# Top-k attention and capped experts on one core: mask products ahead of the second score products, and the signed-score product moved from GpSimd to VectorE

## The chip, the cores and the metric

One core of one Trainium2 chip runs the whole program. TensorE (PE) multiplies matrices, VectorE (DVE) searches and compares, ScalarE (ACT) evaluates exponentials and signs and copies out of PSUM, GpSimd (POOL) does elementwise work on SBUF, SyncE (SP) issues the DMAs. The metric is the device time of one execution in microseconds. The median of the runs is compared; the profile is of one execution.

## The reference

Attention over 8 batches, 8 heads, 576 positions and head size 64, in which each row keeps only its 32 largest scores, followed by a layer of 8 experts that each take at most 80 tokens.

```python
scores = scale * np.matmul(q, k.transpose(0, 1, 3, 2))            # 8 x 8 x 576 x 576
kth = np.partition(scores, -top_k, axis=-1)[..., -top_k:-top_k + 1]   # top_k = 32
scores = np.where(scores >= kth, scores, -1e9)
attn = np.exp(scores - scores.max(-1)); attn /= attn.sum(-1) + 1e-09
x = matmul(attn, v)                                               # -> (4608, 512)
logits = x @ w_gate; expert_idx = argmax(logits); gate_w = softmax(logits)[expert_idx]
for e in range(8):                                                # at most 80 tokens each, by gate_w
    out[tok_idx] = gate_w[tok_idx] * (np.maximum(x[tok_idx] @ w1[e], 0) @ w2[e])
```

## The kernel before

The attention works through 32 head pairs (two heads of one batch, side by side in the 128 partitions as 64 + 64). The 576 query rows of a pair are four blocks of 128 rows and a tail of 64. A unit is one head's block of 128 rows; the tail rows of both heads share one unit. So a pair has nine units, and the attention has 288. `run` issues one step for each unit in a fixed order (`manual_schedule`: each engine executes its instructions in the order written). Within a step the work of several units is staggered:

- `front` (lines 180 to 195): PE computes the score products of a block of both heads (line 190), ACT copies them out of PSUM as `s` (line 195). It is issued two steps ahead of its use.
- `parts` (line 202): six MAX8 over sixths of a row give 48 candidates.
- `search`: three rounds of MAX8 (line 213) and two of MATCH_REPLACE (line 222) on the candidates give the 24th largest, `w9[:, 7]`. ACT then computes the sign of (that value minus s), with its sum over the row in `cnt` (line 218). GpSimd multiplies s by that sign (line 219), which makes the scores above the 24th negative. A MAX8 of the product (line 224) gives the eight next ones, and `pick` (line 227) takes the 32nd by the count.
- `drop` (line 249): VectorE writes `mask`, 1 where s is below the threshold, plus a constant of the row, in bf16.
- `turn_w` (lines 252 to 273): PE computes the scores a second time, transposed (keys by queries, line 269, f32, one head in partitions 0 to 63 and the other in 64 to 127), on top of a product of the mask with a scaled negative identity (line 265, bf16, all 128 partitions), which adds a very large negative number where the key is dropped. The sums lie in PSUM tiles `ab` (four chunks of 128 keys for each head) and `cc` (the last 64 keys of both heads). ACT then takes the exponential of it (lines 272 and 273) as `wT`. In the order before, each chunk of 128 keys has its two mask products and then its two score products, and then the next chunk follows.
- `back` (line 287): PE multiplies `wT` with the values; ACT copies the result out (line 289).
- `norm` (lines 293 to 331) divides, stores, transposes and multiplies with the gate's weights, once in a head pair. GpSimd does the division's products (line 304).

Within a step the order of VectorE's instructions is written as a string, `"GbGcGdGehGmGga"`. G is one of the six `parts` MAX8 of the step's own unit; every other letter is the next piece of `search` of a unit that the table `back` places 0 to 3 steps behind: b to e the rounds (1 step behind), g the MAX8 of the product (2 behind), h and m `pick` and the mask (3 behind). After VectorE's string the step issues `turn_w` of the block whose mask has just been written, then `front` (or the transposes of the next pair's q and k), then `back` of an earlier block. These three share PE in that order, and `front`'s PSUM tile `sp` and `turn_w`'s `ab` have one buffer each. After the attention `judge` tests a bound and `finish` routes the tokens and runs the experts; the change does not touch them.

Of the kernel before, what the change touches and what calls it, by code (L numbers as in the profile page):

```python
# [14 lines left out]
Alu = mybir.AluOpType  # L15
# [9 lines left out]
def kernel(  # L25
# [11 lines left out]
    nc = tc.nc  # L37
    B, H, S, D = q.shape
# [8 lines left out]
    P = 128  # L47
    HP = H // 2
    NP = B * HP
    NF = S // P  # L50
    TL = S - NF * P
    NK = NF + 1
# [60 lines left out]
    class Attention:  # L113
# [92 lines left out]
        def search(self, i):  # L206

            s, cand = self.s[i], self.top[i]
            top = self.top[i] = self.small.tile([P, G0 // 8 - 1, 8], F32, name="top", tag="top")
            w9 = self.small.tile([P, 16], F32, name="w9", tag="w9")  # L210
            for r in range(G0 // 8):
                dst = top[:, r, :] if r < G0 // 8 - 1 else w9[:, :8]
                nc.vector.max(out=dst, in_=cand)  # L213
                if r == G0 // 8 - 1:

                    y = self.rows.tile([P, S], F32, name="y", tag="y", bufs=3)
                    cnt = self.small.tile([P, 1], F32, name="cnt", tag="cnt")
                    nc.scalar.activation(y, s, Act.Sign, bias=w9[:, 7:8], scale=-1.0, accum_out=cnt)  # L218
                    nc.gpsimd.tensor_tensor(out=y, in0=s, in1=y, op=Alu.mult)  # L219
                yield  # L220
                if r < G0 // 8 - 1:
                    nc.vector.match_replace(out=cand, in_to_replace=dst, in_values=cand, imm_value=LOW)  # L222
                    yield
            nc.vector.max(out=w9[:, 8:], in_=y)  # L224
            yield
            pick = self.small.tile([P, TOP_K - G0 + 1], F32, name="pick", tag="pick")
            nc.vector.scalar_tensor_tensor(out=pick, in0=past, scalar=cnt, in1=w9[:, 7:], accum_out=self.thr[:, i : i + 1],  # L227
                                           op0=Alu.is_equal, op1=Alu.mult)
            yield
            self.drop(i)  # L230
            yield
# [19 lines left out]
        def turn_w(self, n, t):  # L251

            qT, kT = self.turned[n]
            i = n * UPP + 2 * t
            m = P if t < NF else TL
            masks = [self.mask.pop(i), self.mask.pop(i + 1)] if t < NF else [self.mask.pop(i)] * 2
            eye = [minus, minus] if t < NF else [minus[:, :TL], minus[:, TL:]]
            ab = self.ps_w.tile([P, 2, NF, P], F32, name="ab", tag="ab")
            cc = self.ps_c.tile([P, 512], F32, name="cc", tag="cc")
            rows = slice(t * P, t * P + m)  # L260
            for c in range(NK):
                ks = slice(c * P, min(c * P + P, S))
                for h in range(2):
                    d = slice(D * h, D * h + D)
                    nc.tensor.matmul(ab[:, h, c, :m] if c < NF else cc[d, :m], lhsT=masks[h][:, ks], rhs=eye[h],  # L265
                                     start=True, stop=False)
                for h in range(2):
                    d = slice(D * h, D * h + D)
                    nc.tensor.matmul(ab[:, h, c, :m] if c < NF else cc[d, :m], lhsT=kT[d, ks], rhs=qT[d, rows],  # L269
                                     start=False, stop=True)  # L270
            wT = self.rows.tile([P, 2 * NF + 1, P], F32, name="wT", tag="wT")
            nc.scalar.activation(wT[:, : 2 * NF, :m], ab.rearrange("p h c r -> p (h c) r")[:, :, :m], Act.Exp, scale=scale)  # L272
            nc.scalar.activation(wT[:, 2 * NF, :m], cc[:, :m], Act.Exp, scale=scale)
            self.w[n, t] = wT, cc
# [93 lines left out]
        def run(self, slow):  # L368

            units = []  # L370
            for n in range(NP):
                for t in range(NF):
                    units += [(n, t, 0), (n, t, 1)]
                units.append((n, NF, 2))
            first, second = {}, {}
            later = []
            due = []

            def step(i):
                if i < NU:  # L380
                    n, t, h = units[i]
                    if t == 0 and h == 1 and 0 < n and n + 1 < NP:
                        self.load(n + 1, *divmod(n + 1, HP))
                    if t in (1, 3) and h == 0 and slow and n:
                        slow.pop(0)()
                    if t == 1 and h == 0 and n + 1 < NP:
                        due.append(n + 1)
                    first[i] = self.parts(i)

                back = dict(a=0, b=1, c=1, d=1, e=1, g=2, h=3, m=3)  # L390
                for c in "GbGcGdGehGmGga":
                    if c == "G":
                        if i < NU:
                            next(first[i])
                    elif c == "a":
                        if i < NU:
                            next(first[i], None)
                            second[i] = self.search(i)
                            next(second[i])
                    elif i - back[c] in second:  # L400
                        next(second[i - back[c]])
                j = i - 3
                if 0 <= j < NU and units[j][2]:
                    self.turn_w(*units[j][:2])
                self.fronts = i + 2 < NU and units[i + 2][2] != 1
                if self.fronts:
                    self.front(*units[i + 2][:2])
                elif due:
                    self.turn(due.pop())
                j = i - 4  # L410
                if 0 <= j < NU and units[j][2]:
                    self.back(*units[j][:2])
                for g in list(later):
                    if next(g, 0) == 0:
                        later.remove(g)
                if 0 <= j < NU and units[j][2] == 2:
                    n = units[j][0]
                    b, hp = divmod(n, HP)
                    later.append(self.norm(n, b, hp, b % 2, 2))

            with tc.manual_schedule():
                self.load(0, 0, 0)
                self.load(1, *divmod(1, HP))
                nc.sync.dma_start(wg, moe_w_gate.rearrange("(c p) e -> p c e", p=P))
                self.turn(0)
                self.front(0, 0)
                i = 0
                while i < NU + 4 or later:
                    step(i)
                    i += 1  # L430
            assert not slow and not due
# [273 lines left out]
```

## Time and profile before

| | before |
|---|---|
| median of 3 runs | 1617.32 us (1616.72 to 1620.83) |
| profiled execution | 1612.21 us, span 1610.5 us |
| PE busy | 1311.5 us, 81% of the span |
| VectorE busy | 1124.7 us, 70% |
| ScalarE busy | 682.4 us, 42% |
| GpSimd busy | 513.0 us, 32% |
| mean granted TensorE clock | 0.826 |

Busy time is the time in which an engine has an instruction under way; waiting is not counted. The granted clock is given as a share of full speed: 1.0 is 2.4 GHz, 0.5 is 1.2 GHz. A timeline row has the start in us from the span's start, the duration in us, the engine, the line of the kernel, the operation, the tiles written and read with their shapes, the number of merged instructions, and in brackets the idle time before it with what ended it. A row of waits has the waiting engine and line, what it waited for, the total in us, the number of waits and the longest. A row of a window has the stretch, its length, the busy time of PE, PE's weight loads, DVE, ACT and POOL with the numbers of instructions, the granted clock, the share of the DMA engines and GB/s.

### The profile page before, as it was taken

The page shows a single profiled execution, that of the slowest core. Times are in us where ns is not written, and L with a number is a line of the kernel's source. Part 1 is how long each engine was busy: PE and PEld are TensorE (multiplying, and loading weights), DVE is VectorE, ACT ScalarE, POOL GpSimd, SP SyncE. Part 2 cuts the span into 40 slices and gives each one's busy share as a digit, 9 for nine tenths or more (in the row PEclk, how much of TensorE's full clock was granted, in tenths as well). Part 3 has the DMA queues.
Part 4 walks back from the last instruction along what each step waited for, and adds up shares of the span by engine and source line. Part 5 has one row for each costly group of instructions (what it writes and reads, how often), then busy time and mean ns, then how long its engine had stood idle before and what let it go on. Part 6 is the DMA issues. An engine that isn't in the chain of part 4 may idle for free.

```text
span 1610.5 us, 38356 instructions
## 1 busy us (share of the span) xinstructions
PE 1311.5 (81%) x14862; PEld 936.5 (58%) x14862; DVE 1124.7 (70%) x5095; ACT 682.4 (42%) x1374; POOL 513.0 (32%) x501
## 2 busy tenths in 40 slices
PE   6889888888888888888888888888888888861787
PEld 4556555555555665555555556655555556550687
DVE  5777777777777777786777777777877777838211
ACT  3454444444444544444444445444444444420010
POOL 2333333333333333333333332333333333320111
PEclk9888788887888887888878888878888788775699
DMA  4022222222111122222221111111111110021270
GB/s 119 9 76 83 83 69 57 57 57 57 38 43 42 49 57 56 57 57 57 57 57 32 46 29 26 31 31 31 31 31 31 31 31 9 9 73 39 74 289 25
DMA packets 154591, 85.94 MB, mean 53 GB/s; under 512 B 118304, under 2 KB 136736, under 8 KB 154400
## 3 DMA queue, kind: packets, MB, share of 16 engines
q1 hardware_dynamic: 153376, 80.78, 17.6%
q0 software_dynamic: 1024, 2.62, 0.5%
q8 instruction: 118, 1.93, 0.5%
q14 instruction: 73, 0.60, 0.1%
HBM read 63.19 MB, written 20.19 MB: 52 GB/s over the span
## 4 chain that ended last, share of the span: by engine, by line
PE 70%; DVE 17%; ACT 11%; issue 2%; POOL 0%; DMA 0%; POOLq 0%; DVEq 0%; ACTq 0%
PE ab L269 19%; PE sp L190 15%; PE ab L265 9%; PE cc L287 9%; ACT s L195 5%; DVE mask L249 4%; DVE cand L202 4%; PE cc L269 4%; DVE pick L227 3%; PE sp L165 3%; PE lp L322 2%; PE yp L613 2%; ACT wT L272 2%; DVE cand L222 2%; PE cc L265 2%
## 5 line engine op out<-in xcount | busy, mean ns | idle before, releaser
L219 POOL TENSOR_TENSOR y<-s,y 128x576 f32<-128x576 f32 x288 | 416.7, 1447 | 891.9 <-ACT y L218 888.1
L202 DVE MAX8 cand<-s 128x8 f32<-128x96 f32 x1728 | 428.7, 248 | 253.2 <-ACT s L195 253.1
L269 PE MATMUL ab<-qT,kT 64*128 64x128 f32 (+1 forms) x2560 | 359.2, 363 | 0.0
L272 ACT ACTIVATE wT<-ab 128x1024 f32<-128x1024 f32 (+1 forms) x160 | 150.2, 939 | 415.8 <-PE ab L269 413.7
L265 PE MATMUL ab<-minus,mask 128*128 128x128 bf16 (+1 forms) x1280 | 197.8, 233 | 150.7 <-DVE mask L249 132.2
L190 PE MATMUL sp<-kT,qT 64*128 64x288 f32 (+1 forms) x1280 | 275.3, 565 | 48.3 <-ACT s L195 25.7
L224 DVE MAX8 w<-y 128x8 f32<-128x576 f32 x288 | 214.6, 745 | 92.9 <-POOL y L219 92.9
L269 PEld LDWEIGHTS ab<-qT,kT 64*128 64x128 f32 x2560 | 228.1, 218 | 68.5 <-issue 18.5
L249 DVE TENSOR_SCALAR mask<-s,thr,top 128x576 bf16<-128x576 f32 x288 | 264.9, 920 | 0.3
L265 PEld LDWEIGHTS <-mask 128*128 128x128 bf16 (+1 forms) x1600 | 103.8, 104 | 255.7 <-DVE mask L249 145.7
L287 PEld LDWEIGHTS cc<-vb,wT 128*64 128x64 f32 x4608 | 210.5, 163 | 67.2 <-issue 52.7
L195 ACT ACTIVATE s<-sp 128x1152 f32<-128x1152 f32 (+1 forms) x160 | 165.7, 1035 | 181.0 <-PE sp L190 180.8
L287 PE MATMUL cc<-vb,wT 128*64 128x65 f32 x4608 | 241.6, 251 | 0.0
L218 ACT ACTIVATE y<-s,w 128x576 f32<-128x576 f32 x288 | 222.8, 774 | 18.7 <-DVE w L213 18.6
L190 PEld LDWEIGHTS sp<-kT,qT 64*128 64x128 f32 (+1 forms) x1280 | 140.6, 233 | 128.9 <-ACT s L195 55.8
L227 DVE SCALAR_TENSOR_TENSOR pick<-past,cnt,w 128x9 f32<-128x9 f32 x288 | 140.4, 487 | 0.2
L222 DVE MATCH_REPLACE8 cand<-top,cand 128x48 f32<-128x48 f32 x576 | 110.2, 191 | 0.0
L213 DVE MAX8 top<-cand 128x8 f32<-128x48 f32 x576 | 110.0, 191 | 0.1
L287 PE MATMUL cc<-vr,wT 128*64 128x65 f32 x1152 | 101.8, 245 | 0.0
L269 PE MATMUL cc<-qT,kT 64*64 64x128 f32 (+1 forms) x640 | 79.7, 335 | 0.0
L289 ACT COPY xu<-cc 128x130 f32<-128x130 f32 (+1 forms) x160 | 42.3, 265 | 80.2 <-PE cc L287 80.1
L287 PEld LDWEIGHTS cc<-vr,wT 128*64 128x64 f32 x1152 | 74.8, 161 | 0.0
(165 smaller groups left out, 991.3 us busy)
## 6 DMA issues: line engine op xcount, KB each, us to landing
w<-in_moe_w_dram SPq DMA_DIRECT2D x32, 512.0 KB, 4.5
w<-in_moe_w_dram SPq DMA_DIRECT2D x8, 2048.0 KB, 11.9
out_dram<-zero SPq DMA_DIRECT2D x9, 1024.0 KB, 8.3
qn<-in_q_dram SPq DMA_DIRECT2D x64, 128.0 KB, 2.7
kn<-in_k_dram SPq DMA_DIRECT2D x64, 128.0 KB, 2.7
vb<-in_v_dram SPq DMA_DIRECT2D x64, 128.0 KB, 2.4
xd<-xn SPq DMA_DIRECT2D x32, 256.0 KB, 2.4
qn<-in_q_dram SPq DMA_DIRECT2D x32, 32.0 KB, 2.5
```

The lines of the kernel that those rows point to most:

```text
L190: nc.tensor.matmul(o, lhsT=qT[d, t * P : t * P + m], rhs=kT[d, j * HS : (j + 1) * HS], start=True, stop=True)
L195: nc.scalar.activation(s[:, : g * S].rearrange("p (j c) -> p j c", c=HS), ps[:, : 2 * g, :HS], Act.Copy, scale=TINY)
L202: nc.vector.max(out=cand[:, j, :], in_=s[:, j * S // NG : (j + 1) * S // NG])
L218: nc.scalar.activation(y, s, Act.Sign, bias=w9[:, 7:8], scale=-1.0, accum_out=cnt)
L219: nc.gpsimd.tensor_tensor(out=y, in0=s, in1=y, op=Alu.mult)
L224: nc.vector.max(out=w9[:, 8:], in_=y)
L227: nc.vector.scalar_tensor_tensor(out=pick, in0=past, scalar=cnt, in1=w9[:, 7:], accum_out=self.thr[:, i : i + 1], op0=Alu.is_equal, op1=Al ...
L249: nc.vector.tensor_scalar(self.mask[i], s, self.thr[:, i : i + 1], top[:, 0, 0:1], op0=Alu.is_lt, op1=Alu.add)
L265: nc.tensor.matmul(ab[:, h, c, :m] if c < NF else cc[d, :m], lhsT=masks[h][:, ks], rhs=eye[h], start=True, stop=False)
L269: nc.tensor.matmul(ab[:, h, c, :m] if c < NF else cc[d, :m], lhsT=kT[d, ks], rhs=qT[d, rows], start=False, stop=True)
L272: nc.scalar.activation(wT[:, : 2 * NF, :m], ab.rearrange("p h c r -> p (h c) r")[:, :, :m], Act.Exp, scale=scale)
L287: nc.tensor.matmul(cc[r : r + TL, o], lhsT=wT[:, h * NF + c if c < NF else 2 * NF, r : r + TL], rhs=vb[:, c, h, :] if c < NF else vr[:, h, ...
```

## The change

In `turn_w` all mask products of a block come first (five for the one head, five for the other), and then all second score products, chunk by chunk. Only the first mask product into each PSUM bank of a head carries the start flag. In `search` the product of the scores with their sign is made by VectorE in place of GpSimd, as a piece of its own (letter y, two steps behind, after the mask and before the last of the six `parts`).

```diff
                     nc.scalar.activation(y, s, Act.Sign, bias=w9[:, 7:8], scale=-1.0, accum_out=cnt)
-                    nc.gpsimd.tensor_tensor(out=y, in0=s, in1=y, op=Alu.mult)
                 yield
                 if r < G0 // 8 - 1:
                     nc.vector.match_replace(out=cand, in_to_replace=dst, in_values=cand, imm_value=LOW)
                     yield
+            nc.vector.tensor_tensor(out=y, in0=s, in1=y, op=Alu.mult)
+            yield
             nc.vector.max(out=w9[:, 8:], in_=y)
...
+            keys = [slice(c * P, min(c * P + P, S)) for c in range(NK)]
+            heads = [slice(D * h, D * h + D) for h in range(2)]
+            dst = [[ab[:, h, c, :m] for c in range(NF)] + [cc[heads[h], :m]] for h in range(2)]
+
+            for h in range(2):
+                for c in range(NK):
+                    nc.tensor.matmul(dst[h][c], lhsT=masks[h][:, keys[c]], rhs=eye[h], start=c in (0, NF), stop=False,
+                                     skip_group_check=True)
             for c in range(NK):
-                ks = slice(c * P, min(c * P + P, S))
                 for h in range(2):
-                    d = slice(D * h, D * h + D)
-                    nc.tensor.matmul(ab[:, h, c, :m] if c < NF else cc[d, :m], lhsT=masks[h][:, ks], rhs=eye[h],
-                                     start=True, stop=False)
-                for h in range(2):
-                    d = slice(D * h, D * h + D)
-                    nc.tensor.matmul(ab[:, h, c, :m] if c < NF else cc[d, :m], lhsT=kT[d, ks], rhs=qT[d, rows],
-                                     start=False, stop=True)
+                    nc.tensor.matmul(dst[h][c], lhsT=kT[heads[h], keys[c]], rhs=qT[heads[h], rows], start=False, stop=True,
+                                     skip_group_check=True)
...
-                back = dict(a=0, b=1, c=1, d=1, e=1, g=2, h=3, m=3)
-                for c in "GbGcGdGehGmGga":
+                back = dict(a=0, b=1, c=1, d=1, e=1, y=2, g=2, h=3, m=3)
+                for c in "GbGcGdGehGmyGga":
```

## The prediction

> **What bounds the kernel now.** I read the page first (busy shares, granted clock, the chain that ended last), then the waits, then one head pair by windows, then the timeline of that pair.
>
> ```profile
> PE 1311.5 (81%) x14862; PEld 936.5 (58%) x14862; DVE 1124.7 (70%) x5095; ACT 682.4 (42%) x1374; POOL 513.0 (32%) x501
> PE 70%; DVE 17%; ACT 11%; issue 2%; POOL 0%; DMA 0%; POOLq 0%; DVEq 0%; ACTq 0%
> PE ab L269 19%; PE sp L190 15%; PE ab L265 9%; PE cc L287 9%; ACT s L195 5%; DVE mask L249 4%; DVE cand L202 4%; PE cc L269 4%; DVE pick L227 3%; PE sp L165 3%; PE lp L322 2%; PE yp L613 2%; ACT wT L272 2%; DVE cand L222 2%; PE cc L265 2%
> ```
> ```profile
> DVE cand L202 <- ACT s L195: 253.1, 93, 8.7
> PE ab L265 <- DVE mask L249: 132.2, 54, 3.9
> DVE w L224 <- POOL y L219: 92.9, 73, 4.0
> ```
>
> The chain runs mostly through PE, and 34% of the span (19 + 9 + 4 + 2) lies on lines 265 and 269, the very block that is reordered. GpSimd is not on the chain at all. VectorE waits for new scores (253 us), which PE delivers late; PE waits for masks (132 us). So the attention is a ring: mask, second scores, the next first scores, ACT's copy, search, mask. One pair of the steady state, a stretch of it at either clock, and the attention as a whole:
>
> ```profile
> 797.16:842.37 45.21, 38.32 (x399) 26.62 (x396) 34.86 (x162) 20.91 (x42) 15.07 (x13) 0.81 0.22 57
> 797.30:810.97 13.67, 12.12 (x139) 8.67 (x140) 12.53 (x66) 7.90 (x17) 4.96 (x4) 1.00 0.27 82
> 831.45:841.68 10.23, 9.48 (x64) 5.56 (x62) 6.72 (x35) 3.62 (x6) 2.08 (x3) 0.50 0.56 124
> 40.00:1427.00 1387.00, 1170.65 (x12371) 815.13 (x12369) 1042.17 (x4864) 653.56 (x1316) 481.96 (x441) 0.83 0.16 44
> ```
>
> The attention fills the window from 40 to 1427 us: about 31 pairs of 44.7 us. In the pair shown PE is busy 38.3 of 45.2 us, VectorE 34.9. The clock is at its upper level, 2.4 GHz (1.00), in the second row and at its lower, 1.2 GHz (0.50), in the third; the pair's mean of 0.81 means that 38% of it pass at the lower level. Nothing of the change reaches the last 180 us.
>
> **The block on PE, before and after.** Timeline of PE at the upper clock, and then at the lower:
>
> ```profile
> 802.26 1.24 PE L190 MATMUL sp<-kT,qT 64*128 64x288 f32 x8 [0.73 <-ACT xT L317]
> ...
> 804.07 0.64 PE L287 MATMUL cc<-vb,wT 128*64 128x65 f32 x16
> 804.53 0.29 PE L287 MATMUL cc<-vr,wT 128*64 128x65 f32 x4
> ...
> 806.51 0.28 PE L265 MATMUL ab<-minus,mask 128*128 128x128 bf16 x2
> 806.73 0.49 PE L269 MATMUL ab<-qT,kT 64*128 64x128 f32 x4
> 807.15 0.29 PE L265 MATMUL ab<-minus,mask 128*128 128x128 bf16 x2
> ...
> 808.43 0.25 PE L265 MATMUL cc<-minus,mask 128*64 128x128 bf16 x2
> 808.61 0.44 PE L269 MATMUL cc<-qT,kT 64*64 64x128 f32 x4
> 809.62 0.22 PE L265 MATMUL ab<-minus,mask 128*128 128x64 bf16 x2 [0.58 <-ACT wT L272]
> 809.77 0.44 PE L269 MATMUL ab<-qT,kT 64*128 64x64 f32 x4
> ```
> ```profile
> 832.59 0.40 PE L265 MATMUL ab<-minus,mask 128*128 128x128 bf16 x2
> 832.92 0.80 PE L269 MATMUL ab<-qT,kT 64*128 64x128 f32 x4
> 833.65 0.40 PE L265 MATMUL ab<-minus,mask 128*128 128x128 bf16 x2
> ...
> 835.44 2.13 PE L190 MATMUL sp<-kT,qT 64*64 64x288 f32 x8
> ```
>
> Now a chunk takes 0.64 us (806.51 to 807.15): 0.22 for two mask products and 0.42 for the score products of two heads, two passes each (x4). Four chunks and the last (0.18, and some 0.36 until the next operation can start) make 3.10 us. No mask product or score pass is added or taken away; what changes is how often PE turns from one kind to the other, ten times before and once after.
>
> What a score pass costs in a row, I take from line 287, which also runs f32 with a load for each product: 16 products on two halves of the columns, so eight passes of 65 columns, in 0.46 us (804.07 to 804.53), or 0.88 ns a column. Line 190 agrees: four passes of 288 columns in 1.24 us with its first load and its last drain. So a pass of 128 columns takes 0.113 us, and two passes 0.23 against the 0.42 of now; the other 0.19 is a load that hides behind nothing and a drain. Ten passes in a row are 1.13 us plus 0.30 for the first load and the end. For mask products, 128 columns against 64 cost 0.22 and 0.15 us a pair (809.62 to 809.77): 0.035 for 64 columns, so 0.07 each and 0.08 fixed for a turn. Ten in a row: 0.78. The new block is 0.78 + 1.13 + 0.30 = 2.2 us; the saving is 0.9, and up to 1.1 if the turn's cost is all hidden; I take 1.0. The bounds: zero, if each load still waits for the product before it, and 1.1. At the lower clock a chunk takes 1.06 us (832.59 to 833.65); with passes of 0.21 (2.13 us for four of 288, scaled) and mask products of 0.12 the same sum saves 1.2. A tail block moves 64 columns but has the same loads and turns: 0.9. One pair, with three full blocks at the upper clock, one at the lower, and a tail: 3.0 + 1.2 + 0.9 = 5.1 us.
>
> The Trainium skill, page "TensorE: Matmul & The Clock Gate", section "What overlaps and what doesn't", speaks against this: a weight load overlaps a running product only where the row groups differ, and the mask products use all rows. By it neither kind would gain from standing in a row, and the sum would keep only the terms of the two parts below. The trace does not agree: the products of line 287 have 128 rows too, and their loads are hidden in the 0.46 us.
>
> **The product on VectorE, and GpSimd silent.**
>
> ```profile
> 802.62 0.21 DVE L227 SCALAR_TENSOR_TENSOR pick<-past,cnt,w 128x9 f32<-128x9 f32 x1
> 802.94 0.58 DVE L249 TENSOR_SCALAR mask<-s,thr,top 128x576 bf16<-128x576 f32 x1
> 807.11 1.40 POOL L219 TENSOR_TENSOR y<-s,y 128x576 f32<-128x576 f32 x1 [2.31 <-ACT y L218]
> 807.16 1.67 DVE L249 TENSOR_SCALAR mask<-s,thr,top 128x576 bf16<-128x576 f32 x1
> 808.92 0.74 DVE L224 MAX8 w<-y 128x8 f32<-128x576 f32 x1
> 809.58 0.19 DVE L213 MAX8 top<-cand 128x8 f32<-128x48 f32 x1
> ```
> ```profile
> L249 DVE TENSOR_SCALAR mask<-s,thr,top 128x576 bf16<-128x576 f32 x288 | 264.9, 920 | 0.3
> L227 DVE SCALAR_TENSOR_TENSOR pick<-past,cnt,w 128x9 f32<-128x9 f32 x288 | 140.4, 487 | 0.2
> L550 DVE TENSOR_TENSOR hot<-slot,iot 128x800 f32<-128x800 f32 x4 | 3.9, 989 | 3.7 <-PE acc L553 3.7
> ```
> ```profile
> 828.04 1.00 DVE L227 SCALAR_TENSOR_TENSOR pick<-past,cnt,w 128x9 f32<-128x9 f32 x1
> 829.16 1.72 DVE L249 TENSOR_SCALAR mask<-s,thr,top 128x576 bf16<-128x576 f32 x1
> ```
> ```profile
> 830.93 0.23 PE L265 MATMUL ab<-minus,mask 128*128 128x128 bf16 x1 [3.85 <-DVE mask L249]
> ```
>
> The same mask takes 0.58 us alone and 1.67 when a GpSimd product starts beside it; `pick` takes 0.21 or 1.00. Their means are 0.920 and 0.487, so GpSimd's presence costs VectorE 288 x (0.34 + 0.28) = 178 us. With line 219 gone from POOL this goes; the divisions of `norm` stay (one in a pair). Added are 288 products on VectorE. An f32 product of 800 columns takes 0.989, of 576 therefore 0.71 to 0.76; a MAX8 over 576 shows 0.74 and lets the next start after 0.66 (808.92 to 809.58). I take 0.67; ends 0.6 and 1.40 (GpSimd's own). 288 x 0.67 = 193 us. VectorE's total thus hardly moves (+15), but the time moves to another place: from ahead of the mask to behind it. Per pair, 34.86 - 9 x 0.62 + 9 x 0.67 = 35.3 us.
>
> What is queued behind the new product: one piece of `parts`, the MAX8 of line 224 and the next step. What it waits for, ACT's sign, was issued a step earlier, and now no 1.40 us of GpSimd stands between; the 93 us of waits on POOL y end, and I count nothing for them, since PE's queue covers them. The mask does get earlier. In the pair shown PE stands idle for 3.85 us at 830.93, because the second head's mask is late by the long `pick` (0.79 over) and the long mask (1.14 over): 1.9 us come back there. Once in a pair, as the 132 us of this wait (4.1 a pair) say. Issues of DMAs are untouched, and SP and POOL are moved past nothing.
>
> **The sum.** Per pair 5.1 + 1.9 = 7.0 us, over 32 pairs 224, from 1612 (the profiled execution) to 1388. Next to be late is VectorE: 44.7 - 7.0 = 37.7 leaves it 2.4 us idle in a pair where now it waits 7.9 for scores (253 / 32). At the lower clock it must still wait for some: the loop there (a block of 3.8, first scores of 2.1, and ACT's copy) is longer than its own work between mask and next scores. I give back 1 us a pair, between none and 2.5: 32 us, 1420. The profiled execution was 5 us faster than the median of the runs, so about 1420 to 1425 in their terms; I say 1420. The likeliest case's own range is 1365 to 1475.
>
> **Rivals.**
> 1. The clock falls less often. Now it falls twice in the pair, once behind the 3.85 us of idle PE. If only one fall remained, the 17 us at the lower clock (38% of 45.2) would be about half, PE would rarely hold VectorE up, and VectorE's 35.3 us would be the limit: 9.2 us a pair, 1612 - 294 = 1318. Against it: the fall at 810.97 comes with PE busy 12.12 of 13.67 us. The Trainium skill, same page, section "Why this matters for your kernels", asks for no long idle gaps between bursts of matmuls; by that rule the second fall goes and the first needs another reason, so the trace bears it out by half.
> 2. Loads are hidden only in part (half the saving of a block, 2.6 a pair): 1612 - 32 x (2.6 + 1.9 - 0.8) = 1495.
> 3. VectorE's added product lies on the ring wholly: 7.0 - 6.0 = 1.0 us a pair, 1580. For it: 35.3 of 37.7 us busy. Against it: the product stands behind the mask, and VectorE waits there for scores anyway.
> 4. The change hardly acts, within 0.3%: the block saves nothing and VectorE takes the mask's gain: 1612 to 1617.
> 5. Slower: denser bursts and longer rests hold the clock at 0.50. Then five blocks of 3.8, five first scores of 2.1, five `back` of 2.3 (0.46 and 0.12 us for a head's products in the rows above, two heads, twice as long) and by estimate 5.5 of transposes and gate products fill 46.5 us a pair on PE alone, 1.8 more than now: 1612 + 58 = 1670. At the upper clock the same list is about 26 us, so it decides from some nine tenths of the work at the lower clock; the pair now has 38% of its time there. Against it: at 0.50 PE is nearly always busy (9.48 of 10.23), and the clock has risen each time.
>
> **How the numbers follow.** Chances: forecast 0.47, rival 1 0.18, rival 2 0.17, rival 3 0.09, rival 4 0.04, rival 5 0.05. The range of 1300 to 1510 holds the forecast and the first two rivals, 0.82. About 0.3% (5 us) is what these runs can tell from no change. Faster 0.91, same 0.04, slower 0.05.
>
> **What would show it.** After the change the timeline should show ten mask products in about 0.8 us and the twenty score passes in about 1.3, a block of 2.2 us; the mask at 0.58 and `pick` at 0.21 in nearly all 288; the product at 0.71 to 0.76; no wait for POOL y; PE's wait for masks spread over more blocks, each short; POOL busy under 100 us. I'd be wrong by the block if its rows keep 0.42 us for a chunk's scores, by the ring if PE's waits for masks grow beyond 350 us, by the clock if its mean leaves 0.75 to 0.9.

## Result and profile after

| | before | after |
|---|---|---|
| median | 1617.15 us | 1345.53 us |
| ratio | | 0.832 (0.829 to 0.835) |
| profiled execution, span | 1610.5 us | 1341.7 us |
| attention, to the last mask | 1427 us | 1159 us |
| mean granted clock | 0.826 | 0.908 |

All of the gain lies in the attention (268 us between the two profiled executions); what follows it takes 183 us in both. The page of the changed kernel, with busy time, granted clock and the chain that ended last:

```profile
PE 1081.9 (81%) x14862; PEld 834.7 (62%) x14862; DVE 1127.2 (84%) x5383; ACT 679.1 (51%) x1374; POOL 91.8 (7%) x213
PEclk9998989999889899898899989898898998855899
PE 47%; DVE 41%; ACT 8%; issue 2%; POOL 0%; DMA 0%; POOLq 0%; DVEq 0%; ACTq 0%
PE sp L190 11%; DVE cand L202 10%; PE ab L272 9%; DVE mask L250 8%; PE cc L290 7%; DVE y L223 6%; DVE w L225 6%; DVE cand L221 4%; PE ab L268 4%; ACT s L195 4%; PE yp L616 3%; PE cc L272 3%; DVE top L213 2%; PE cc L268 2%; PE sp L165 2%
```

VectorE's busy time has not moved (1124.7 and 1127.2 us) while its share of the chain went from 17% to 41%. The two lines of the block (268 and 272 now) hold 18% of the chain where they held 34%. The attention as one window, and the waits of the ring:

```profile
40.00:1159.00 1119.00, 942.22 (x12311) 712.95 (x12312) 1041.26 (x5132) 646.22 (x1309) 69.24 (x159) 0.93 0.20 55
```
```profile
PE ab L268 <- DVE mask L250: 106.9, 91, 2.4
DVE cand L202 <- ACT s L195: 76.2, 57, 8.8
```

VectorE is active for 1041 of 1119 us (before: 1042 of 1387), and waits 76 us for scores instead of 253. The wait for POOL's product is gone from the list. PE still waits 107 us for masks, but in 91 waits of at most 2.4 us in place of 54 of up to 3.9. A clock of 0.93 in this row means 14% of the attention at 1.2 GHz, 157 us; 0.83 before means 34%, 471 us. The block at the upper clock, in the timeline of PE:

```profile
604.26 0.40 PE L268 MATMUL ab<-minus,mask 128*128 128x128 bf16 x4 [1.58 <-DVE mask L250]
...
610.50 0.40 PE L268 MATMUL ab<-minus,mask 128*128 128x128 bf16 x4
610.82 0.24 PE L268 MATMUL cc<-minus,mask 128*64 128x128 bf16 x1
611.55 0.40 PE L268 MATMUL ab<-minus,mask 128*128 128x128 bf16 x4 [0.48 <-DVE mask L250]
...
634.49 0.40 PE L268 MATMUL ab<-minus,mask 128*128 128x128 bf16 x4
634.81 0.24 PE L268 MATMUL cc<-minus,mask 128*64 128x128 bf16 x1
634.99 0.40 PE L268 MATMUL ab<-minus,mask 128*128 128x128 bf16 x4
635.32 0.24 PE L268 MATMUL cc<-minus,mask 128*64 128x128 bf16 x1
635.49 1.16 PE L272 MATMUL ab<-qT,kT 64*128 64x128 f32 x16
636.58 0.43 PE L272 MATMUL cc<-qT,kT 64*64 64x128 f32 x4
636.95 1.24 PE L190 MATMUL sp<-kT,qT 64*128 64x288 f32 x8
```

It takes 2.46 us (634.49 to 636.95) where it took 3.10. Four mask products need 0.32 us up to the start of the next, and the one for the last 64 keys 0.17 to 0.18, where one more product of the same shape takes some 0.056 (56 in 3.14 us, below): a turn between products of 128 and of 64 columns takes as long as about three products, and there are five such turns. The two products for the last 64 keys, one of each head, stood together before and took 0.18 us (808.43 to 808.61 in the prediction's rows); the new order parts them, and each takes as long as the two did. The score passes of four chunks take 1.09 us.

The new order does one more thing. Before, PE could issue one mask product of the first head and then rested until the second head's mask was there, as this row and the one of 830.93 in the prediction show; now all five of the first head (610.50 to 611.06) run ahead of that wait:

```profile
826.85 0.23 PE L265 MATMUL ab<-minus,mask 128*128 128x128 bf16 x1
```

Three of VectorE's own groups, and PE's loads of the masks (busy us, mean ns):

```profile
L223 DVE TENSOR_TENSOR y<-s,y 128x576 f32<-128x576 f32 x288 | 216.6, 752 | 3.4 <-ACT y L218 1.4
L250 DVE TENSOR_SCALAR mask<-s,thr,top 128x576 bf16<-128x576 f32 x288 | 166.8, 579 | 1.5 <-DVE cand L202 0.6 <-PE ab L272 0.3 <-PE cc L268 0.3
L228 DVE SCALAR_TENSOR_TENSOR pick<-past,cnt,w 128x9 f32<-128x9 f32 x288 | 61.6, 214 | 0.1
L268 PEld LDWEIGHTS <-mask 128*128 128x128 bf16 (+1 forms) x1600 | 106.2, 101 | 168.2 <-DVE mask L250 122.1
```

### The profile page after: what moved, and what is told of

It reads as the page before. It is cut to its first block, busy times and chain, and to the rows that moved or that the text cites. A ratio compares the mean times of both kernels' runs of the same rounds, so it can differ in the third digit from the quotient of the medians.

```text
span 1341.7 us, 38270 instructions
## 1 busy us (share of the span) xinstructions
PE 1081.9 (81%) x14862; PEld 834.7 (62%) x14862; DVE 1127.2 (84%) x5383; ACT 679.1 (51%) x1374; POOL 91.8 (7%) x213
## 4 chain that ended last, share of the span: by engine, by line
PE 47%; DVE 41%; ACT 8%; issue 2%; POOL 0%; DMA 0%; POOLq 0%; DVEq 0%; ACTq 0%
PE sp L190 11%; DVE cand L202 10%; PE ab L272 9%; DVE mask L250 8%; PE cc L290 7%; DVE y L223 6%; DVE w L225 6%; DVE cand L221 4%; PE ab L268 4%; ACT s L195 4%; PE yp L616 3%; PE cc L272 3%; DVE top L213 2%; PE cc L268 2%; PE sp L165 2%
## 5 line engine op out<-in xcount | busy, mean ns | idle before, releaser
L190 PE MATMUL sp<-kT,qT 64*128 64x288 f32 (+1 forms) x1280 | 233.0, 490 | 48.3 <-ACT s L195 25.7
L290 PEld LDWEIGHTS cc<-vb,wT 128*64 128x64 f32 x4608 | 197.7, 153 | 62.2 <-issue 47.2
L290 PE MATMUL cc<-vb,wT 128*64 128x65 f32 x4608 | 227.2, 241 | 0.0
L223 DVE TENSOR_TENSOR y<-s,y 128x576 f32<-128x576 f32 x288 | 216.6, 752 | 3.4 <-ACT y L218 1.4
L268 PE MATMUL ab<-minus,mask 128*128 128x128 bf16 (+1 forms) x1280 | 120.1, 216 | 110.0 <-DVE mask L250 106.9
L272 PE MATMUL ab<-qT,kT 64*128 64x128 f32 (+1 forms) x2560 | 193.3, 293 | 0.0
L190 PEld LDWEIGHTS sp<-kT,qT 64*128 64x128 f32 (+1 forms) x1280 | 122.3, 204 | 106.1 <-ACT s L195 44.4
L272 PEld LDWEIGHTS ab<-qT,kT 64*128 64x128 f32 x2560 | 163.6, 196 | 10.0
L250 DVE TENSOR_SCALAR mask<-s,thr,top 128x576 bf16<-128x576 f32 x288 | 166.8, 579 | 1.5 <-DVE cand L202 0.6
L268 PE MATMUL cc<-minus,mask 128*64 128x128 bf16 (+1 forms) x320 | 76.3, 238 | 0.0
```

What stands on the lines that cost most here:

```text
L190: nc.tensor.matmul(o, lhsT=qT[d, t * P : t * P + m], rhs=kT[d, j * HS : (j + 1) * HS], start=True, stop=True)
L223: nc.vector.tensor_tensor(out=y, in0=s, in1=y, op=Alu.mult)
L250: nc.vector.tensor_scalar(self.mask[i], s, self.thr[:, i : i + 1], top[:, 0, 0:1], op0=Alu.is_lt, op1=Alu.add)
L268: nc.tensor.matmul(dst[h][c], lhsT=masks[h][:, keys[c]], rhs=eye[h], start=c in (0, NF), stop=False, skip_group_check=True)
L272: nc.tensor.matmul(dst[h][c], lhsT=kT[heads[h], keys[c]], rhs=qT[heads[h], rows], start=False, stop=True, skip_group_check=True)
L290: nc.tensor.matmul(cc[r : r + TL, o], lhsT=wT[:, h * NF + c if c < NF else 2 * NF, r : r + TL], rhs=vb[:, c, h, :] if c < NF else vr[:, h, ...
```

## Experiments

The theory at the start (A): the gain needs both parts, and moves the limit to VectorE. The rival (B): PE's order and the clock are the whole of it. Medians of all runs:

| kernel | us | ratio to before, interval |
|---|---|---|
| order on PE alone | 1420.2 | 0.878 (0.877 to 0.880) |
| product on VectorE alone | 1495.0 | 0.923 (0.919 to 0.926) |
| changed, and an idle product on GpSimd | 1386.7 | 0.858 (0.853 to 0.862) |
| changed, and a second operation on VectorE | 1504.6 | 0.931 (0.928 to 0.934) |
| changed, first scores ahead of the block | 1273.3 | 0.788 (0.786 to 0.790) |
| changed, last 64 keys' mask products together | 1310.1 | 0.810 (0.808 to 0.812) |
| both of these | 1269.8 | 0.786 (0.784 to 0.788) |
| before, with idle PE products | 1477.5 | 0.913 (0.909 to 0.916) |
| changed, with idle PE products | 1290.3 | 0.798 (0.796 to 0.800) |
| order alone, with idle PE products | 1325.5 | 0.820 (0.819 to 0.822) |
| both moves, 160 of 288 masks on ACT | 1224.1 | 0.757 (0.755 to 0.759) |
| both moves, all masks on ACT | 1422.2 | 0.879 (0.876 to 0.883) |

**Each part alone.** The order:

```diff
 nc.scalar.activation(y, s, Act.Sign, bias=w9[:, 7:8], scale=-1.0, accum_out=cnt)
+nc.gpsimd.tensor_tensor(out=y, in0=s, in1=y, op=Alu.mult)      # and no product on VectorE
```

> Only the order on PE is changed; the product stays on GpSimd. Theory A (the gain of 272 us needs both parts: PE's shorter block moves the limit to VectorE, and VectorE can only take it because GpSimd no longer holds it up): a block takes 2.46 us at the upper clock, 160 x 0.64 = 102 us come back and a little of the time at the lower clock, so 1470 to 1510; the mask stays near 0.92 and pick near 0.49 on average; time at the lower clock between 300 and 450 us of the attention. Theory B (the order on PE is the whole gain, by itself and through the clock): 1340 to 1400, lower clock under 200 us.

The product, with the loops of `turn_w` as they were:

```diff
-nc.gpsimd.tensor_tensor(out=y, in0=s, in1=y, op=Alu.mult)
+nc.vector.tensor_tensor(out=y, in0=s, in1=y, op=Alu.mult)      # letter y, as in the change
```

> Only the product is moved to VectorE; PE keeps mask and score products in turn. Theory A: the 1.9 us of late mask in a pair come back, about 60 us, and the block stays at 3.10 to 3.17 us: 1530 to 1570; mask 0.58 and pick 0.21 in all; VectorE's active time as before (1042 us), time at the lower clock above 350 us. Theory B: 1600 to 1620, since VectorE's total work is the same and PE's is unchanged.

Their attention windows, the order first, then the mask and `pick` with the order alone, and PE's wait for masks with the product alone:

```profile
40.00:1237.00 1197.00, 986.80 (x12359) 742.52 (x12357) 1044.77 (x4861) 647.04 (x1313) 475.39 (x441) 0.89 0.19 51
```
```profile
40.00:1316.00 1276.00, 1126.55 (x12371) 791.66 (x12367) 1052.71 (x5146) 652.86 (x1316) 69.81 (x159) 0.86 0.18 48
```
```profile
L249 DVE TENSOR_SCALAR mask<-s,thr,top 128x576 bf16<-128x576 f32 x288 | 231.4, 803 | 0.3
L227 DVE SCALAR_TENSOR_TENSOR pick<-past,cnt,w 128x9 f32<-128x9 f32 x288 | 183.4, 637 | 0.2
```
```profile
PE ab L266 <- DVE mask L250: 65.5, 35, 1.9
```

The order gives 197 us by itself, the product 123; together 272 and not 320, so 48 us are shared. Both beat theory A's forecasts, and the order falls short of B: the gain does not need both parts, each brings time by itself. In both the clock rose (0.83 to 0.89 and 0.86): time at the lower level is about 265 us (22% of 1197) and 365 us (29% of 1276) against 471. With the product alone PE's wait for masks is halved (132 to 66 us) and its longest rest for one is 1.9 us in place of 3.9, and most of the time at the lower level stays: the shorter rest alone does not keep the clock up there. With GpSimd's product still there, the stretched instructions stay as costly in sum (mask 0.80, `pick` 0.64), though they change places.

**Does the presence of GpSimd cost the time?**

```diff
 nc.scalar.activation(y, s, Act.Sign, bias=w9[:, 7:8], scale=-1.0, accum_out=cnt)
+nc.gpsimd.tensor_tensor(out=zero, in0=zero, in1=cnt.to_broadcast([P, Dm]), op=Alu.mult)
```

> The changed kernel with a product on GpSimd beside it that nobody waits for: 512 columns of a tile of zeros by cnt, written in place, started by the end of ACT's sign as the product was before. If GpSimd's presence alone is what cost VectorE 178 us, the mask's mean goes from 0.58 to 0.8 or more and pick's from 0.21 to 0.4 or more, and as VectorE is the limit (1041 of 1119 us) the time rises by 100 to 160 us, to 1445 to 1505. Rival: PE is still the limit and VectorE's stretching is hidden: under 1375. Second rival: what was lost before was the wait for GpSimd's result and not the stretched instructions: under 1360 with the mask still stretched.

Groups of VectorE:

```profile
L224 DVE TENSOR_TENSOR y<-s,y 128x576 f32<-128x576 f32 x288 | 238.8, 829 | 1.1 <-ACT y L218 0.3
L251 DVE TENSOR_SCALAR mask<-s,thr,top 128x576 bf16<-128x576 f32 x288 | 169.3, 588 | 1.5 <-DVE cand L202 0.9 <-PE cc L273 0.3
L229 DVE SCALAR_TENSOR_TENSOR pick<-past,cnt,w 128x9 f32<-128x9 f32 x288 | 97.5, 338 | 0.1
```

The time rose by 41 us, between the numbers of the theories. GpSimd's presence does stretch VectorE's instructions with nobody waiting for it (`pick` 0.21 to 0.34, the product 0.75 to 0.83), but the mask hardly. What is stretched depends on how the two meet. In the traces a mask is long where a GpSimd product already runs when it starts, or starts within 0.1 us of it: 86 of 288 in the kernel before, 1.72 us on average, and 3 here. Another 40 here were 0.37 us or more under way when a GpSimd product started, and took 0.58. The new product was caught 27 times (1.58). The added GpSimd product is also shorter than the old one (1.15 us on average, before 1.45). So 178 us is what GpSimd cost in the kernel before, not a constant.

**Is VectorE the limit?**

```diff
 nc.vector.tensor_tensor(out=y, in0=s, in1=y, op=Alu.mult)
+nc.vector.tensor_tensor(out=y, in0=y, in1=y, op=Alu.max)
```

> The changed kernel with a second f32 operation of two tensors on VectorE behind the product (the maximum of y with itself, 0.75 us long, 0.67 to the next start). If VectorE is the limit, 288 x 0.67 = 193 us less a part of its 78 us of waits come on top: 1470 to 1540. If PE and the ring through it are the limit, the second operation falls into VectorE's waits: under 1400. The mask's length does not change in either.

```profile
40.00:1315.00 1275.00, 1027.01 (x12373) 773.44 (x12373) 1255.10 (x5430) 656.75 (x1313) 69.33 (x159) 0.86 0.18 48
```

VectorE works 214 us more and the time rises by 159, as forecast for the limit: it is now active for 1255 of 1275 us, PE rests more, and the clock is back at 0.86. One more operation per unit on VectorE takes back more than half of what the change brought.

**What the order on PE still holds up.** First the next scores ahead of the block (the code is shortened here), then a mask order with one turn to 64 columns, then both:

```diff
+if self.fronts: self.front(*units[i + 2][:2])
+elif due: self.turn(due.pop())
 if 0 <= j < NU and units[j][2]: self.turn_w(*units[j][:2])
-if self.fronts: self.front(*units[i + 2][:2])
-elif due: self.turn(due.pop())
```

> The changed kernel with one more move: in each step the next first scores (or the transposes of the next pair) are issued ahead of the block of mask and second score products, so that PE can do them while it waits for the mask. If VectorE's remaining 78 us of waits for scores come from the order on PE, they nearly vanish: VectorE's waits under 30 us and the time 1285 to 1320. Rival: the waits come from ACT's queue or from PE's time at the lower clock and stay: 1335 to 1355. Second rival: the block now starts later behind the first scores, and exponentials and values fall behind: over 1360.

```diff
-for h in range(2):
-    for c in range(NK):
+for cs in (range(NF), range(NF, NK)):
+    for h in range(2):
+        for c in cs:
```

> The changed kernel with the mask products of both heads' four large chunks first and the two of the last 64 keys behind them, so that PE turns from 128 to 64 columns once and not twice. The block, 2.46 us with 0.15 to 0.17 us at each turn, should take about 2.15 us. If VectorE is the limit this hardly moves the time: 1325 to 1348. If PE's path is the limit, 160 x 0.3 = 48 us: under 1305.

> Both moves, first scores ahead and one turn to 64 columns. VectorE's 1041 us of work are the floor of the attention, which now takes 1119: 1280 to 1310 if that is the limit; the second move adds at most 10 us to what the first gives. If PE's path still counts, 20 us or more below the first move alone.

The windows of the first and, from the second, the block in the timeline of PE:

```profile
40.00:1092.00 1052.00, 912.64 (x12307) 689.16 (x12306) 1038.75 (x5128) 636.77 (x1307) 75.72 (x159) 0.95 0.21 58
```
```profile
616.44 0.62 PE L269 MATMUL ab<-minus,mask 128*128 128x128 bf16 x8
616.99 0.25 PE L269 MATMUL cc<-minus,mask 128*64 128x128 bf16 x2
617.16 1.16 PE L273 MATMUL ab<-qT,kT 64*128 64x128 f32 x16
618.26 0.44 PE L273 MATMUL cc<-qT,kT 64*64 64x128 f32 x4
618.62 1.24 PE L190 MATMUL sp<-kT,qT 64*128 64x288 f32 x8
```

With the first scores ahead, VectorE is active for 1039 of 1052 us: most of the 72 us that went are its waits (1119 - 1041 = 78 us became 13), and 1273 is below the 1285 to 1320 that were expected. PE's order had made these waits, but not by itself: with the clock held instead (below) they also fall, to 1067 - 1039 = 28 us. The other move shortens the block to 2.18 us (616.44 to 618.62), as the two products for the last 64 keys stand together again (0.17 for both) and two changes of shape are gone. It gives 35 us, more than the theory that VectorE alone is the limit grants (at most 20) and less than if all lay on PE (48). Together they give 76, some 4 more than the first alone, which the intervals do not tell from nothing; 1270 is below the 1280 to 1310 expected. With the first move, PE's block hardly counts any more.

**What is the clock worth?** Idle products that nobody reads, in PE's rest ahead of the second block of each pair, in the kernel before and in the changed one:

```diff
 rows = slice(t * P, t * P + m)
+if t == 1 and not self.lean:
+    for _ in range(56):
+        nc.tensor.matmul(cc[:, 384:512], lhsT=minus, rhs=minus, start=True, stop=True)
```

> The kernel before with 56 bf16 products of the scaled identity with itself, into columns that nobody reads, issued ahead of the second block of each pair: PE works there through some 3 of the 3.85 us in which it rests for the second head's mask. If the rest is what lets the clock fall at that place, one of the two falls in a pair goes: time at the lower clock from 470 to 200 to 300 us, and the time falls by 30 to 90 us although work is added. Rival: the clock falls whatever PE does there: lower-clock time above 420 us and the time 1615 to 1660.

> The changed kernel with the same 56 idle products of PE ahead of the second block of each pair. Without the change they were worth 140 us, through the clock. If the change has taken most of that itself (lower-clock time 160 us of the attention, where it was 470) and VectorE, which the clock does not touch, is the limit, they bring little or cost their own 3 us a pair: 1320 to 1365. Rival: the clock still holds up the ring as much as it did: under 1300.

The kernel before with them: its attention window, and the place of the long rest in PE's timeline; then the window of the changed kernel with them.

```profile
40.00:1292.00 1252.00, 1126.63 (x14091) 828.78 (x14087) 1055.51 (x4863) 650.16 (x1315) 481.41 (x441) 0.95 0.18 49
```
```profile
829.89 3.30 PE L263 MATMUL cc<-minus 128*128 128x128 bf16 x56
833.03 0.22 PE L268 MATMUL ab<-minus,mask 128*128 128x128 bf16 x1
833.99 0.23 PE L268 MATMUL ab<-minus,mask 128*128 128x128 bf16 x1 [0.74 <-DVE mask L249]
```
```profile
40.00:1107.00 1067.00, 966.69 (x14080) 763.74 (x14075) 1039.04 (x5130) 647.28 (x1311) 66.07 (x159) 1.00 0.21 57
```

Adding 3.1 us of useless work to each pair of the kernel before takes 138 us off it, more than the 30 to 90 expected. The rest for the mask shrinks from 3.85 to 0.74 us, the clock goes from 0.83 to 0.95, and the time at the lower level from 471 to 125 us. So the lower clock cost the kernel before half as much as the whole change gave. In the changed kernel the clock hardly falls any more (1.00 in the row), and 55 us come off: the rival was right there, the clock still held up the ring. Between the two kernels with idle products the change gives 187 us (1477.5 to 1290.3), without them 272. By this difference some 85 us of its gain, about a third, came through the clock; that is an estimate, as the clock is 0.95 in the one and 1.00 in the other.

> Only the order on PE changed (product on GpSimd), with the 56 idle products of PE ahead of the second block of each pair. It stands between two kernels with the same idle products: the one before (1477) and the changed one (1290). If the order's worth at a held clock is the block's own shortening, 160 x 0.64 = 102 us come off 1477: 1365 to 1390, and the product's move is worth some 85 us more. If the order had its 197 us mostly through the block: under 1330. If it had them mostly through the clock, which is held here: over 1410.

The order alone with the same products, its window:

```profile
40.00:1140.00 1100.00, 985.88 (x14059) 773.72 (x14055) 1037.65 (x4851) 645.48 (x1310) 471.08 (x440) 0.98 0.20 56
```

So with the products in all three, the order brings 152 us (1477.5 to 1325.5), which is more than 160 x 0.64 = 102, and the product's move 35 more. 1326 misses the first forecast, is under the 1330 of the second (mostly through the block), and is far from the third (over 1410). PE's busy time is 141 us lower (1126.6 to 985.9). By estimate some 40 us of that are the clock, which differs even here (0.95 and 0.98 mean 125 and 44 us at the lower level, at half speed), and the rest is about the block's 102. What the order gives beyond these isn't settled: the first head's mask products now run ahead of a wait, and the shorter block also lets masks, scores and copies meet otherwise. That was not tried apart.

**A version that beats both.** With both moves, masks of the first head and of the tail made by ACT as Relu of threshold minus score, times an identity scaled by another 2^40; the row's largest score is not subtracted in this version. Then all masks there.

```diff
-nc.vector.tensor_scalar(self.mask[i], s, self.thr[:, i : i + 1], top[:, 0, 0:1], op0=Alu.is_lt, op1=Alu.add)
+if i % UPP % 2 == 0:                                   # always, in the second version
+    nc.scalar.activation(self.mask[i], s, Act.Relu, bias=self.thr[:, i : i + 1], scale=-1.0)
+else:
+    nc.vector.tensor_scalar(self.mask[i], s, self.thr[:, i : i + 1], None, op0=Alu.is_lt)
```

> The version with first scores ahead and one turn, and the masks of the first head and of the tail (160 of 288) made by ACT (Relu of threshold minus score, times a larger negative identity) and no longer by VectorE; the row's largest score is no longer subtracted before the exponential. VectorE, which waits for 10 us only in 1049, loses 160 x 0.49 = 78 us; ACT gains 160 x 0.78 = 125 to about 760. If VectorE is the one limit: 1190 to 1215. Rival: ACT's queue now lies on the way from threshold to mask and holds up the ring: over 1235.

> As the version with half the masks on ACT, with all 288 masks there. VectorE loses 288 x 0.49 = 141 us (to about 900), ACT gains 225 (to about 860), PE has 881 at hand: three engines near 900. If limits simply add up engine by engine: 1130 to 1170. More likely ACT's order (masks between signs, exponentials and copies) holds up the ring: 1180 to 1260; over 1270 if the mask's way through ACT costs more than VectorE gains.

The window of the first, and a wait of the second:

```profile
40.00:1040.00 1000.00, 860.26 (x12284) 661.82 (x12281) 949.60 (x4968) 736.91 (x1463) 65.90 (x159) 0.97 0.22 61
```
```profile
DVE y L223 <- ACT y L218: 259.8, 176, 3.5
```

Half the masks on ACT take 90 us off VectorE and 46 off the time: 1224.1 us, the fastest kernel here, between the two forecasts. All masks on ACT bring VectorE to waiting 260 us for ACT's signs (6 with the two moves alone), which now stand in ACT's queue among masks, and the clock is lower too (0.88 over the execution, 0.94 with half the masks): 1422, far over the 1270 of the worst case that was expected.

## Why the prediction was right, and where its sizes were off

The direction, VectorE as the engine next to be late and the single costs came as written: the product measured 0.752 us (0.71 to 0.76 forecast), the mask 0.579, `pick` 0.214, a score pass in the row 0.112 from start to start (0.113), VectorE's total unchanged, POOL under 100 us. 1346 lies inside the stated range, but 74 us below the forecast and below the forecast's own range (1365 to 1475), nearer to rival 1's 1318. What rival 1 describes came beside what I forecast: the time at the lower level fell to a third, and the traces have 31 stretches of it in the attention where there were 63, about one in a pair in place of two. The stated range held because it took that rival in; and the steps below missed in both directions, so that the sum came as near as it did is in part luck. By its steps:

- *The block.* Forecast 2.2 us, measured 2.46. The ten score passes came as forecast (1.46 us, 1.43 in the sum), so their loads are hidden, and rival 2 is not what took from the gain; the ten mask products took 1.00 and not 0.78. I counted one turn's cost; the rows show one at each change between 128 and 64 columns as well, and the two products for the last 64 keys no longer stand together. Putting these together again made the block 2.18. The term was 0.64 and not 1.0 us a block, by that number 102 us in place of 163.
- *The late mask.* Forecast 61 us for the product's move; alone it gave 123. I had taken only the one long rest of each pair (the row that I read as one wait a pair has 54 waits, not 32) and set the 93 us of waits for POOL's product at nothing. How the further 62 us divide between these waits, the other stretched masks and the clock is open.
- *The clock.* This is the term I sized worst: I left the share at the lower level as it was, and gave its fall 0.18 as a rival. It went from 34% to 14%, by the estimate above some 85 us of the gain, and my own mark for being wrong by it (a mean outside 0.75 to 0.9) was passed with 0.908. Filling the rest of 3.85 us with idle products took most of the falls away and 138 us off the kernel before. My argument against the rival, that the clock also fell with PE 89% busy, did not hold: with the rest filled, falls at other places went too (125 us at the lower level are left, far less than half of 471). Whether the missing rest or the added products did it was not tried apart; the product alone, with no rest for a mask over 1.9 us and the clock at 0.86, speaks against the rest alone.
- *What is given back.* Forecast 1 us a pair for VectorE's near limit. VectorE does come within 78 us of its limit, and the second operation shows it; but I took its need as 35.3 us a pair from one pair, while the whole attention gives 1041 / 31 = 33.6, so there was more room.

Of the rivals, the third (the product wholly on the ring) fell with the product alone: 123 us faster. The fifth, a clock held low, did not come in the changed kernel, though with the second operation on VectorE it went back to 0.86. The Trainium skill's rule in "TensorE: Matmul & The Clock Gate", section "What overlaps and what doesn't", by which full-row loads would hide behind nothing, does not agree with the rows: 56 full-row products with a load each take 0.056 us apiece, and four mask products up to the next start 0.32, while one load of a mask takes 0.101 on average. My "neither kind" read the rule too far besides: the two heads' score products use different halves of the rows, so it would have granted them an overlap. That page's advice against long idle gaps, section "Why this matters for your kernels", agrees with the runs as far as they go: filling the gap took the clock from 0.83 to 0.95.

## What to carry to other kernels

Look at what an engine does before its clock falls, and price the fall before pricing instructions: here 3.1 us of unread products, once in some 45, brought half as much as the whole change. When two engines are near their limit, the order of a shared queue decides: work that waits for nobody (the next scores) belongs ahead of work that waits. Sort small matrix products by their shape as well as by their kind, and count the turns between shapes.

## What was not expected of the hardware

Useless matrix products made a kernel faster by 138 us (8.5%). A GpSimd product beside VectorE stretched the mask from 0.58 to 1.67 us and `pick` from 0.21 to 1.00 us in the kernel before, yet with the idle GpSimd product beside the changed kernel the mask was hardly hit (0.588 mean) and the new product was (0.829). The turn between products of 128 and of 64 columns took 0.15 to 0.18 us from start to start (0.32 - 3 x 0.056 in the one direction, 0.17 to 0.18 in the other), against 0.056 for one more product of the same shape (56 in 3.14 us); and two products of 64 columns, one of each head, side by side took no longer than one.
